# An output projection made of seven products of halves in place of eight, and the three products of a hidden block kept together, in an f32 kernel of attention and MLP

## The chip, the cores and the metric

One of the eight cores of a Trainium2 chip. The time is device microseconds (us) of one execution. The engines: TensorE (PE: matmuls; PEld: its loads of weights, which overlap the matmuls), VectorE (DVE), ScalarE (ACT), GpSimd (POOL), SyncE (SP, which issues DMAs here).

## The reference, cut to what matters

An HGRN2 attention over 4 x 768 tokens and 8 heads of 48 gives x of 3072 x 384. An MLP follows; the change touches only its last product.

```python
def _moe_ref(x, w_in, w_out):
    h = x @ w_in                                   # 3072 x 384 @ 384 x 2048
    g = h * (1.0 / (1.0 + np.exp(-1.702 * h)))
    return (g @ w_out).astype(np.float32)          # 3072 x 2048 @ 2048 x 384
```

Everything is f32.

## The kernel before

Tokens are taken in 12 units of 256. Each unit has an attention part (many small matmuls of 48 or 64 rows, which wait for each other through VectorE and ScalarE) and an MLP part (large matmuls, which wait for little). TensorE's order is written by hand: between two attention parts it runs a measured share of the MLP of an older unit, so that the large matmuls fill the attention's waits. VectorE's and ScalarE's order in the late part is a scheduler's. Units 0 to 2 go through the MLP in blocks while w_in and w_out are still being fetched and turned from f64 to f32; units 3 to 11, the late ones, run whole.

```python
    def mlp_h(n, ffs, g):                 # h of one 128-row block: three products over c
        def one(ff, c):
            ...
            nc.tensor.matmul(ph, lhsT=w_in[:, c, ff * P:(ff + 1) * P], rhs=xTs[n][:, c, :], start=(c == 0), stop=(c == NK - 1))
            if c == NK - 1:
                nc.scalar.activation(sg, ph, AF.Sigmoid, scale=1.702)
                nc.vector.tensor_tensor(g[ff // FG][:, ff % FG, :], ph, sg, ALU.mult)
        return [(U, lambda ff=ff, c=c: one(ff, c), ...) for ff in ffs for c in range(NK)]

    def mlp_o(n, ffs, g, done):           # o of 128 tokens: 16 products of 384 columns
        def one(tt, ff):
            if ff == ffs[0]:
                t["po"] = ps.tile([P, DM], F32, tag="mm", bufs=4, ...)
            nc.tensor.matmul(t["po"], lhsT=g[ff // FG][:, ff % FG, tt * P:(tt + 1) * P], rhs=w_out[:, ff, :],
                             start=(ff == ffs[0]), stop=(ff == ffs[-1]))
            if ff == ffs[-1]:
                done(tt, t["po"])         # ScalarE copies po out, then the store
        ...
```

The h, the o and some attention transposes take turns on four PSUM banks (tag "mm"). [Cuts are marked with "...".]

Of the kernel before, what the change touches and what calls it, by code (L numbers as in the profile page):

```python
# [9 lines left out]
F32 = mybir.dt.float32  # L10
I32 = mybir.dt.int32
U32 = mybir.dt.uint32
AF = mybir.ActivationFunctionType
ALU = mybir.AluOpType
# [9 lines left out]
def kernel(  # L24
# [7 lines left out]
    moe_w_out: bass.AP,  # L32
    out: bass.AP,
):



# [19 lines left out]
    nc = tc.nc  # L57
    B, H, S, D = q.shape
    DM = H * D
    DFF = moe_w_in.shape[1]  # L60
    P = 128
    C = 64
    G = 128
    U = 256
# [7 lines left out]
    NK = DM // P  # L72
    NFF = DFF // P
    FG = 4
    PAIRS_AHEAD = 3
# [9 lines left out]
    wp = ctx.enter_context(tc.tile_pool(name="wp", bufs=2))  # L85
    mlp = ctx.enter_context(tc.tile_pool(name="mlp", bufs=2))
    ps = ctx.enter_context(tc.tile_pool(name="ps", bufs=1, space=bass.MemoryType.PSUM))
# [43 lines left out]
    X = const.tile([P, 3, NX], F32, name="X")  # L131
# [8 lines left out]
    w_out = const.tile([P, NFF, DM], F32, name="w_out")  # L140
# [7 lines left out]
    pieces, pairs = [], []  # L148
    for r in range(NGR):
        ffs = range(r * FG, (r + 1) * FG)  # L150
        for ff in ffs[::2]:
            f = slice(ff * P, (ff + 2) * P)
# [8 lines left out]
    NPC = 2 * FG  # L161
# [68 lines left out]
    def convert():  # L230

        if state["begin"] < len(pairs) and len(todo) <= NOP:
            begin_pair(state["begin"])
            state["begin"] += 1
        if todo and todo[0]:
            todo.pop(0)()
        if todo and todo[0] is None:
            todo.pop(0)
            state["done"] += 2
            fetch_weights()  # L240
# [360 lines left out]
        return (begin_f, begin, begin_k, begin_gates), parts  # L601


    xTs = {}

    def width(n):

        return U + (n == NALL - 1)

    def mlp_h(n, ffs, g):  # L610
        t = {}

        def one(ff, c):
            if c == 0:
                if ff % FG == 0:
                    g[ff // FG] = mlp.tile([P, FG, width(n)], F32, tag="g", name=f"g_{n}_{ff}", bufs=6)
                t["ph"] = ps.tile([P, width(n)], F32, tag="mm", name=f"h_{n}_{ff}", bufs=4)
            ph = t["ph"]
            nc.tensor.matmul(  # L619
                ph, lhsT=w_in[:, c, ff * P:(ff + 1) * P], rhs=xTs[n][:, c, :], start=(c == 0), stop=(c == NK - 1)  # L620
            )
            if c == NK - 1:
                sg = mlp.tile([P, width(n)], F32, tag="sg", name=f"sg_{n}_{ff}")
                nc.scalar.activation(sg, ph, AF.Sigmoid, scale=1.702)  # L624
                nc.vector.tensor_tensor(g[ff // FG][:, ff % FG, :], ph, sg, ALU.mult)  # L625
                if width(n) > U:

                    by = g[ff // FG][:, ff % FG, U:]
                    if ff == 0:
                        g["last"] = mlp.tile([P, 1, DM], F32, tag="sum", name="sum_last", bufs=3)  # L630
                        nc.vector.tensor_scalar(g["last"][:, 0], w_out[:, 0, :], by, None, op0=ALU.mult)
                    else:
                        nc.vector.scalar_tensor_tensor(
                            g["last"][:, 0], w_out[:, ff, :], by, g["last"][:, 0], op0=ALU.mult, op1=ALU.add
                        )
        return [(U, lambda ff=ff, c=c: one(ff, c), ff // FG * NPC + ff % FG + 1) for ff in ffs for c in range(NK)]

    def mlp_o(n, ffs, g, done):

        t = {}  # L640

        def one(tt, ff):
            if ff == ffs[0]:
                t["po"] = ps.tile([P, DM], F32, tag="mm", name=f"o_{n}_{tt}_{ff}", bufs=4)
            nc.tensor.matmul(  # L645
                t["po"], lhsT=g[ff // FG][:, ff % FG, tt * P:(tt + 1) * P], rhs=w_out[:, ff, :],
                start=(ff == ffs[0]), stop=(ff == ffs[-1]),
            )
            if ff == ffs[-1]:
                done(tt, t["po"])  # L650
        return [(DM, lambda tt=tt, ff=ff: one(tt, ff), (ff // FG + 1) * NPC) for tt in range(U // P) for ff in ffs]

    def store(n, tt, o):
        r0 = n * U + tt * P - 1
        nc.sync.dma_start(out=out[max(r0, 0):r0 + P, :], in_=o[1:] if r0 < 0 else o)

    def mlp_unit(n):
        g = {}

        def done(tt, po):  # L660
            if tt == 0:
                g["o"] = mlp.tile([P, U // P, DM], F32, tag="osb", name=f"osb_{n}", bufs=1)
            o = g["o"][:, tt]
            nc.scalar.copy(o, po)  # L664
            store(n, tt, o)

        def last_token():
            po = ps.tile([P, DM], F32, tag="mm", name="o_last", bufs=4)
            nc.tensor.matmul(po[:1], lhsT=ones, rhs=g["last"][:, 0], start=True, stop=True)
            nc.scalar.copy(g["last"][:1, 0], po[:1])  # L670
            nc.sync.dma_start(out=out[NALL * U - 1:, :], in_=g["last"][:1, 0])
        o = mlp_o(n, range(NFF), g, done)
        if width(n) > U:
            o.insert(NFF, (DM, last_token, 0))
        return mlp_h(n, range(NFF), g) + o

    sums = {}

    def mlp_block(n, r):

        g, ffs = {}, range(r * FG, (r + 1) * FG)

        def done(tt, po):
            if r == 0 and tt == 0:
                sums[n] = mlp.tile([P, U // P, DM], F32, tag="sum", name=f"sum_{n}", bufs=3)
            acc = sums[n][:, tt]
            if r == 0:
                nc.scalar.copy(acc, po)
            else:
                nc.vector.tensor_tensor(acc, acc, po, ALU.add)  # L690
            if r == NGR - 1:
                store(n, tt, acc)
        return mlp_h(n, ffs, g), mlp_o(n, ffs, g, done)
# [10 lines left out]
    def parts_of(n):  # L704

        parts = list(units[n][1])
        _, inter = parts.pop()
        if n:
            kind, scores = parts[0]
            _, ahead = units[n - 1][1][-1]  # L710
            parts[0] = kind, lambda: (ahead(), scores())
        if n < N_TURN:

            def with_v(l):
                kind, fn = parts[l]
                return kind, lambda: (fn(), load_vl(n, l) if n == 0 or l else None)
            parts[:NL] = [with_v(l) for l in range(NL)]
        if n + 1 < NALL:
            begin_f, begin, begin_k, begin_gates = units[n + 1][0]
            i = len(parts)  # L720
            if n + 1 < N_FILL:

                parts.append(("K", lambda: (begin_k(), begin_gates(), load_vl(n + 1, 0) if n + 1 < N_TURN else None)))
                parts.insert(i - 4, ("B", begin))
                parts.insert(i - 5, ("B", begin_f))
            else:
                kind, states = parts.pop()
                parts += [("B", begin_k), (kind, lambda: (states(), begin_gates()))]
                parts.insert(i - 3, ("B", lambda: (begin_f(), begin())))
        else:  # L730
            parts.append(("W", inter))
        return parts

    def merge(n, fill, columns, share, pieces=0, hold=0, by=1.0):



        parts = parts_of(n)
        total = sum(share(kind) for kind, _ in parts)
        converting = {"W": 3, "T": 3, "B": 1} if n < N_FILL - 1 else {"W": 3, "V": 4, "S": 3, "T": 1, "B": 1}  # L740
        total_ops = sum(converting.get(kind, 0) for kind, _ in parts)
        held = sum(share(kind) for kind, _ in parts[:hold])
        at = at_ops = done = ops = 0
        for kind, fn in parts:
            ready = state["done"]
            fn()
            at += share(kind)
            at_ops += converting.get(kind, 0)
            n_ops = min(int(pieces * NOP * at_ops / (by * total_ops)), pieces * NOP) - ops
            ops += n_ops  # L750
            first, n_columns = done, max(0, columns * (at - held) / (total - held) - done)

            def some(end):
                nonlocal done
                while fill and done < end and fill[0][2] <= ready:
                    w, emit, _ = fill.pop(0)
                    emit()
                    done += w
            for i in range(n_ops):
                some(first + n_columns * i / n_ops)  # L760
                convert()
            some(first + n_columns)
# [4 lines left out]
    UNIT = NFF * NK * U + U // P * NFF * DM  # L767
# [14 lines left out]
    fill = []  # L782
# [8 lines left out]
    for n in range(3, NALL):  # L791
        fill += mlp_unit(n)
    for n in range(4, NALL):
        merge(n, fill, UNIT, steady)
    for _, emit, _ in fill:
        emit()

# [28 lines left out]
```

## Time and profile before

| | before |
|---|---|
| median of the three runs | 677.96 us (677.47 to 679.17) |
| span in the profile | 674.0 us |
| TensorE busy | 652.6 us, 97% |
| VectorE busy | 378.4 us, 56% |
| passes of h, distance from start to start | 216 ns for 256 columns |
| passes of o, distance from start to start | 322 ns for 384 columns |
| one late unit, from the start of an attention y to the next unit's | 50.94 us |

Each attention part has one group of matmuls that adds the old state to its output ("y<-X,st", L562). Its first start, read from the trace, divides the run into twelve stretches. I call these starts y1 to y12. From y5 to y11 they come every 50.94 us in the kernel before, all the same to 0.01 us.

The prediction below shows the lines of the profile and how they are read.

### The profile page before, as it was taken

Reading aid. Unit: us, or ns where it says so; the run is one execution under the profiler, and the core shown is the slowest. Engines: PE = TensorE matmul, PEld = TensorE weight load, DVE = VectorE, ACT = ScalarE, POOL = GpSimd, SP = SyncE. Lnnn points to the kernel's source line nnn. Section 1 sums busy time; section 2 is a strip of 40 time slices with the busy share of each in tenths; the row PEclk is TensorE's granted clock in tenths of the full one; section 3 lists DMA queues with packets and bytes.
Section 4 is the critical chain, followed back from the end, with each engine's and each line's share of the span. In section 5 each row is a group of like instructions: output and inputs, shape, how many; then the busy total and the mean of one; then the engine's idle time right before and its main releaser. Section 6 shows DMA issues by size and latency. Waiting matters only on the chain.

```text
span 674.0 us, 19354 instructions
## 1 busy us (share of the span) xinstructions
PE 652.6 (97%) x8514; PEld 486.5 (72%) x8514; DVE 378.4 (56%) x675; ACT 226.4 (34%) x459; POOL 50.3 (7%) x116
## 2 busy tenths in 40 slices
PE   5879999999999999999999999999999999999997
PEld 4656766757777886886886886876886786786774
DVE  3999877887666546545546546445446444430440
ACT  4564443343134233333333233233233233231210
POOL 3020020010002002002002002002002001000000
PEclk9789999999999999999999999999999999999999
DMA  8877973571063535415415415415414103001000
GB/s 193 226 192 193 240 160 89 152 185 37 24 159 107 154 66 149 109 38 148 115 33 152 110 37 148 113 37 144 115 37 115 37 24 84 15 1 36 13 1 24
DMA packets 67551, 67.62 MB, mean 100 GB/s; under 512 B 30410, under 2 KB 61290, under 8 KB 67466
## 3 DMA queue, kind: packets, MB, share of 16 engines
q1 hardware_dynamic: 67466, 66.38, 38.6%
q8 instruction: 67, 1.10, 0.7%
q14 instruction: 18, 0.15, 0.1%
HBM read 56.92 MB, written 8.65 MB: 97 GB/s over the span
## 4 chain that ended last, share of the span: by engine, by line
PE 89%; DVE 7%; ACT 2%; issue 1%; DMA 1%; SPq 0%; DVEq 0%; ACTq 0%
PE h L619 37%; PE o L645 35%; PE sc L383 5%; PE y L447 5%; PE t L338 2%; PE y L562 2%; PE tkn L504 1%; PE sc L522 1%; DVE s L218 1%; DVE A L409 1%; DMA xT<-yT 1%; PE tv L283 1%; ACT yT L570 1%; DVE X L436 1%; DVE X L438 1%
## 5 line engine op out<-in xcount | busy, mean ns | idle before, releaser
L619 PE MATMUL h<-xT,w_in 128*128 128x256 f32 (+1 forms) x1152 | 261.1, 382 | 1.1 <-DVE sum L690 0.8
L645 PE MATMUL o<-w_out,g 128*128 128x384 f32 x768 | 259.6, 491 | 0.9 <-DVE g L625 0.9
L619 PEld LDWEIGHTS h<-xT,w_in 128*128 128x128 f32 x1152 | 215.8, 190 | 36.8 <-issue 3.5
L645 PEld LDWEIGHTS o<-w_out,g 128*128 128x128 f32 x768 | 143.0, 190 | 94.5 <-issue 2.2
L625 DVE TENSOR_TENSOR g<-h,sg 128x256 f32<-128x256 f32 (+1 forms) x192 | 80.8, 422 | 133.1 <-ACT sg L624 132.6
L624 ACT ACTIVATE sg<-h 128x256 f32<-128x256 f32 (+1 forms) x192 | 73.2, 383 | 169.4 <-PE h L619 164.1
L422 ACT COPY Kc<-X 128x512 f32<-128x512 f32 x69 | 45.9, 666 | 123.7 <-DVE X L438 87.3
L438 DVE TENSOR_TENSOR X<-X,tot 128x1024 f32<-128x1024 f32 x45 | 55.2, 1226 | 54.8 <-PE sc L383 50.1
L409 DVE TENSOR_TENSOR A<-sc,masks 128x512 f32<-128x512 f32 x72 | 46.7, 679 | 0.0
L326 DVE STREAM_TRANSPOSE X<-raw 128x1024 f32<-128x1024 f32 x18 | 36.7, 2039 | 16.7 <-PE y L562 13.9
L447 PE MATMUL y<-A,vl 64*48 64x64 f32 x2304 | 41.7, 219 | 0.0
L447 PEld LDWEIGHTS y<-A,vl 64*48 64x48 f32 x2304 | 36.8, 122 | 5.3 <-issue 5.0
L375 POOL TENSOR_TENSOR tot<-F 128x512 f32<-128x512 f32 x12 | 12.5, 1039 | 340.5 <-DVE st L539 327.9
L383 PE MATMUL sc<-X,Kc 48*64 48x64 f32 x1344 | 29.0, 224 | 6.8 <-ACT Kc L422 4.6
L383 PEld LDWEIGHTS sc<-X,Kc 48*64 48x64 f32 x1344 | 24.6, 138 | 13.8 <-ACT Kc L422 7.2
L570 ACT COPY yT<-y 48x512 f32<-48x512 f32 x48 | 27.8, 580 | 20.0 <-PE y L562 19.4
L331 ACT ACTIVATE F<-F 128x1024 f32<-128x1024 f32 x9 | 9.5, 1057 | 49.0 <-DVE F L326 49.0
L375 POOL TENSOR_TENSOR tot<-tot 128x256 f32<-128x256 f32 (+4 forms) x60 | 23.7, 395 | 4.7
L542 DVE TENSOR_TENSOR st<-st,sc 128x192 f32<-128x192 f32 x44 | 15.6, 354 | 15.1 <-PE sc L522 13.7
L338 PE MATMUL t<-ident,raw 128*64 128x128 f32 x288 | 19.6, 298 | 4.4 <-DMA raw<-in_f_logit_dram 4.4
L338 PEld LDWEIGHTS t<-ident,raw 128*64 128x64 f32 x288 | 18.4, 153 | 7.0 <-issue 6.1
L664 ACT COPY osb<-o 128x384 f32<-128x384 f32 x18 | 8.6, 478 | 41.5 <-PE o L645 41.5
(66 smaller groups left out, 385.0 us busy)
## 6 DMA issues: line engine op xcount, KB each, us to landing
vl<-v_tok SPq DMA_DIRECT2D x60, 192.0 KB, 2.8
bits<-in_moe_w_out_dram SPq DMA_DIRECT2D x8, 768.0 KB, 9.8
bits<-in_moe_w_in_dram SPq DMA_DIRECT2D x8, 576.0 KB, 7.9
v_tok<-in_v_dram SPq DMA_DIRECT2D x10, 384.0 KB, 4.3
vn<-v_tok SPq DMA_DIRECT2D x10, 384.0 KB, 6.0
xT<-yT SPq DMA_DIRECT2D x24, 144.0 KB, 2.7
raw<-in_f_logit_dram SPq DMA_DIRECT2D x18, 192.0 KB, 3.9
raw<-in_q_dram SPq DMA_DIRECT2D x18, 192.0 KB, 3.1
```

The lines of the kernel that those rows point to most:

```text
L326: nc.vector.transpose(out.rearrange("p (a i j) -> p a j i", a=NP, j=R), raw[:, j].rearrange("p a (j d) -> p (a j) d", j=R)[:, :, :32],)
L338: nc.tensor.matmul(pt[h * HS:(h + 1) * HS, jj, :], lhsT=by_pair[j][:, h, x:x + HS], rhs=ident, start=True, stop=True)
L375: nc.gpsimd.tensor_tensor(tn, t2[:, :, 0], t2[:, :, 1], ALU.mult)
L383: nc.tensor.matmul(out[g * HS:(g + 1) * HS, h, a, :], lhsT=lhs(h, a * U + g * G), rhs=rhs(h, a * U + g * G), start=True, stop=True,)
L409: nc.vector.tensor_tensor(A[:, :, c:c + w].rearrange("p h (x t) -> p h x t", t=64), t["sc"][:, :, c:c + w].rearrange("p h (x t) -> p h x t ...
L422: nc.scalar.copy(c.rearrange("p (n m) -> p n m", m=m), X[:, j, :NA].rearrange("p (n two m) -> p n two m", two=2, m=m)[:, :, hf, :],)
L438: nc.vector.tensor_tensor(qk, qk, by, ALU.mult)
L447: nc.tensor.matmul(dst(h, g, a), lhsT=vls[n, u][g * 64:(g + 1) * 64, (2 * a + h) * D:(2 * a + h + 1) * D], rhs=A(h, g, a), start=(start an ...
L619: nc.tensor.matmul(ph, lhsT=w_in[:, c, ff * P:(ff + 1) * P], rhs=xTs[n][:, c, :], start=(c == 0), stop=(c == NK - 1))
L624: nc.scalar.activation(sg, ph, AF.Sigmoid, scale=1.702)
L625: nc.vector.tensor_tensor(g[ff // FG][:, ff % FG, :], ph, sg, ALU.mult)
L645: nc.tensor.matmul(t["po"], lhsT=g[ff // FG][:, ff % FG, tt * P:(tt + 1) * P], rhs=w_out[:, ff, :], start=(ff == ffs[0]), stop=(ff == ffs[ ...
```

## The change

The intent: a product of 2 x 2 blocks by 2 x 2 blocks needs eight products of blocks, or seven with some sums (Strassen's method, here in a form that shares sums). The blocks are two halves of the tokens and two of the 2048 hidden rows in g, and two halves of the hidden rows and two of the 384 columns in w_out. TensorE saves one product in eight; VectorE pays with sums of 128x512 over g in each unit (eight), and once with sums over the quarters of w_out (T1 to T4). Four banks X, W, Y, Z hold the products; three of the four are used twice or added to.

```diff
+    def sums_of_b():                       # T1 to T4, ten sums on VectorE, once
+        sub = lambda *x: nc.vector.tensor_tensor(*x, ALU.subtract)
+        ...
+    def sums_of_a(n, g, b):                # six sums a unit, as the blocks of g arrive
+        if b < 2:
+            tt(g["S", j][:, :, t1], g[j][:, :, t0], g[j][:, :, t1], ALU.subtract)
+        else:
+            tt(g[j][:, :, t1], g[j][:, :, t1], g[j + 2][:, :, t1], ALU.add)
+            tt(g["S", j][:, :, t0], g[j][:, :, t1], g[j][:, :, t0], ALU.subtract)
+    def last_sum(n, g):                    # two more, once the product p2 has read the old block
+        ...
+        def p6():
+            nc.vector.tensor_tensor(row("u2"), t["p1"], t["Y"], ALU.add)
+        def p7():
+            nc.vector.tensor_tensor(row("u3"), t["p1"], t["Y"], ALU.add)
+            ...
+        products = (
+            ("X", a(0, 0), b(0, 0), p1, True), ("W", a(1, 1), T_(4), p4, True), ("X", a(0, 1), b(1, 0), p2, False),
+            ("Y", s(0), T_(2), p6, True), ("Z", a(1, 0), T_(1), p5, True), ("Y", s(1), T_(3), p7, False),
+            ("Z", a(0, 1), b(1, 1), p3, False),
+        )
...
-        return [(U, lambda ff=ff, c=c: one(ff, c), ...) for ff in ffs for c in range(NK)]
+        return [(NK * U, lambda ff=ff: [one(ff, c) for c in range(NK)], ...) for ff in ffs]
...
-        o = mlp_o(n, range(NFF), g, done)
+        o = mlp_o7(n, g)
...
-        return mlp_h(n, range(NFF), g) + o
+        return mlp_h(n, range(NFF), g, True) + o
```

In "products" the last field says whether the product starts a bank afresh (True) or is added to what is there (False). Each is 8 matmuls of 192 columns. Not shown: the share of the MLP that runs between two attention parts is counted anew for the fewer columns, and the program gives out the sums of w_out two at a time in the attention part of unit 4.

## The prediction

> **What bounds the kernel now.** I read the page first, for the share of each engine and for the slices of time:
>
> ```profile
> PE 652.6 (97%) x8514; PEld 486.5 (72%) x8514; DVE 378.4 (56%) x675; ACT 226.4 (34%) x459; POOL 50.3 (7%) x116
> ...
> PE   5879999999999999999999999999999999999997
> PEld 4656766757777886886886886876886786786774
> DVE  3999877887666546545546546445446444430440
> ...
> PE h L619 37%; PE o L645 35%; PE sc L383 5%; PE y L447 5%; PE t L338 2%; PE y L562 2%; PE tkn L504 1%; PE sc L522 1%; DVE s L218 1%; DVE A L409 1%; DMA xT<-yT 1%; PE tv L283 1%; ACT yT L570 1%; DVE X L436 1%; DVE X L438 1%
> ```
>
> TensorE (PE) is at 9 in nearly every slice, and the chain that ended last runs through h (37%) and o (35%), both on TensorE. A busy PE need not be at its peak, so I then took one middle stretch of 51 us, about one unit of 256 tokens, from the busy time by windows:
>
> ```profile
> core 0: us, PE busy (x) PEld busy (x) DVE busy (x) ACT busy (x) POOL busy (x), PEclk, DMA share, GB/s
> 310.00:361.00 51.00, 51.00 (x682) 38.49 (x680) 25.92 (x38) 16.93 (x35) 4.03 (x8) 1.00 0.39 100
> ```
>
> There is no hole in TensorE there and its clock is full; VectorE (DVE) has half the time free. All PE waits over 0.15 us that I found in the trace lie before 152 us. So from there on, a us of TensorE work removed is a us off the end, unless a new wait appears. The cost of one matmul is not its duration (they overlap) but the distance from start to start. The timeline gives it:
>
> ```profile
> 599.21 0.60 PE L504 MATMUL tkn<-ident,X 128*128 128x128 f32 x4
> 599.65 2.32 PE L619 MATMUL h<-xT,w_in 128*128 128x256 f32 x10
> 648.74 10.48 PE L645 MATMUL o<-w_out,g 128*128 128x384 f32 x32
> ```
>
> A run of n lasts (n-1) distances and one duration. For o, with the group's own median duration of 0.486 us: (10.48-0.486)/31 = 322.4 ns for 384 columns. For h: (2.32-0.379)/9 = 215.7 ns for 256. An f32 product is two such passes (the 1152 h records are 12 units x 48 products x 2), so o takes 32 x 2 = 64 passes a unit, 64 x 322.4 = 20.63 us.
>
> **What the Trainium skill says.** "TensorE: Matmul & The Clock Gate", section "Back-to-back issue gap", gives N/2.4 + 2.5 ns per warm matmul. The trace agrees if each f32 pass takes two cycles a column: 2x256/2.4+2.5 = 215.8 and 2x384/2.4+2.5 = 322.5, both within 0.2 ns of what I read. By that line a pass of 192 columns takes 162.5 ns; the straight line through the two measured points gives 162.4. The same page, section "LDWEIGHTS (loading the stationary operand)", gives columns/1.2, 107 ns for 128. The trace seems to differ, for a load is shown with 190 ns:
>
> ```profile
> L619 PEld LDWEIGHTS h<-xT,w_in 128*128 128x128 f32 x1152 | 215.8, 190 | 36.8 <-issue 3.5
> L645 PEld LDWEIGHTS o<-w_out,g 128*128 128x128 f32 x768 | 143.0, 190 | 94.5 <-issue 2.2
> ```
>
> But where h follows the 128-column transposes of k (first pair of lines of the timeline above), the loads start about 109 ns apart, (0.60-0.273)/3, and by single records the first load of h starts at 599.541, its matmul at 599.648, 107 ns later, and the next one comes 219 ns after that, only 3 late. So 190 is a latency, and about 110 ns the pace of loads. A pass of 192 columns hides that.
>
> "VectorE: DVE Perf Modes", section "The TRN2 errata", gives (N+151)/0.96 ns for an f32 tensor_tensor: 691 ns at 512, 357 at 192. The trace has 685 for X<-X,tot at 512 and 354 for the state updates at 192: agreed.
>
> **The change part by part.**
>
> Removed and added on TensorE: for the nine late units (3 to 11), 64 passes of 384 columns become 7 products x 8 blocks x 2 = 112 passes of 192, at 162.5 ns = 18.20 us. Saved 20.63-18.20 = 2.43 us a unit, 21.9 us in nine. All of it lies where PE has no holes. Weights are loaded 112 times instead of 64, hidden as argued. The switches between h or o and the small attention matmuls (about 93 ns lost each: 309 instead of 216 from a last h pass to a first sc) stay as many, one for each part of attention, so I give nothing for the three products of an h kept together; it only stops a half-filled bank from being held over an attention part.
>
> Added on VectorE, a unit: eight sums over 128x512 (8 x 0.69 = 5.5 us) and five over 192 columns (5 x 0.355 = 1.8 us), 7.3 us. ScalarE: four copies of 192 columns for two of 384, some +0.3 us (an estimate). VectorE would be busy 26+7.3 = 33 of about 48.5 us: still not the bound by sum. Once, ten sums of w_out's quarters: 6 of 768 columns and 4 of 384, 6 x 0.96 + 4 x 0.55 = 7.9 us.
>
> Moved: the bound by sum is not enough, because VectorE works in order. I went through the order of instructions of both kernels for each place where TensorE waits for VectorE or ScalarE.
>
> - The fourth accumulator, Y, is used twice: S x T2, then 8 blocks of Z, then S' x T3 added into the same bank. The second use must wait until VectorE has taken the first (u2 = p1+Y). In VectorE's order u2 stands behind: two corrections of a (which wait for the product before the attention's y), the transpose of q, the state, two promotions of X and the mask. In the kernel before, the same row runs like this, o having restarted at 363.37:
>
> ```profile
> 362.58 2.06 DVE L326 STREAM_TRANSPOSE X<-raw 128x1024 f32<-128x1024 f32 x1 [2.12 <-PE y L562]
> 364.49 0.34 DVE L539 TENSOR_TENSOR st<-st,tot 128x192 f32<-128x192 f32 x1
> 364.75 1.20 DVE L438 TENSOR_TENSOR X<-X,tot 128x1024 f32<-128x1024 f32 x1
> 365.88 1.27 DVE L409 TENSOR_TENSOR A<-sc,masks 128x512 f32<-128x512 f32 x2
> 367.32 1.24 DVE L438 TENSOR_TENSOR X<-X,tot 128x1024 f32<-128x1024 f32 x1 [0.17 <-ACT Qc L422]
> ```
>
> It ends at 368.56, 5.2 us after the restart. The two corrections (1.3 us) can start about 1.1 us before y ends and push it by some 0.15 us. Then u2 takes 0.35. So Y is free at 5.2+0.15+0.35 = 5.7 us, while TensorE arrives after 16 blocks x 2 x 0.1625 = 5.2 us: a new wait of 0.5 us. Units 3, 5, 6 and 8 have this; 4 and 7 have no state step in the row (0.3 us less, wait 0.2); 9 has no transpose, 10 and 11 no attention in the way: none. Sum 4 x 0.5 + 2 x 0.2 = 2.4 us.
>
> - X's and Z's second use wait for ScalarE copies that have 2.6 us of other products to run in: none. The four matmul banks: the next unit's first h's take X's and W's, long free; the fourth takes Z's some 3 us after its sum should be done: none.
> - The scheduler draws the sums of w_out up into the early stage, near 153 us, and puts the first two (1.9 us) ahead of the first gelu product of a block, where TensorE already waits for banks that VectorE empties:
>
> ```profile
> PE h L619 <- DVE sum L690: 0.8, 1, 0.8
> ```
>
> I put 1.2 us of new PE wait there (a choice between nothing and the full 1.9); the rest falls in idle VectorE time.
>
> At the end a sum of 192 columns takes the place of a copy of 384 (0.48 us) before the last store: about -0.1, left out. Sum: 677.96 - 21.9 + 2.4 + 1.2 = 659.7 us, a fall of 2.7%.
>
> **The rivals.**
> - Loads become the bound: if the 190 ns were the pace, o would take 112 x 0.190 = 21.3 us a unit, 0.65 more than now, 684 us in all. For: PEld's duration is what the page shows, and nothing of exactly this shape (two-pass f32, 128x128 weights, under 190 ns apart) runs in the kernel but at the transposes' border. Against: that border, and the 109 ns pace of the transposes.
> - VectorE becomes a bound in stretches: the wait for Y grows to 1 us or more in all units, and h's banks are emptied late because of the sums between the gelu products. For: in-order engine, 7 us more, the transposes of 2 us. Against: VectorE idles about 0.9 us of each 1.3 us of h. It would leave a gain of 10 to 14 us, 664 to 668.
> - No new wait: if VectorE's row runs 0.5 us sooner than I think, 656.
> - The early stage (to 152 us, VectorE at 8 or 9 tenths) shifts with the changed order of h, either way by 1 to 2 us.
>
> **Range and chances.** The saving is arithmetic on a well supported pace; the waits can only be 0 to about 8 us. Fast end 655, slow end 666. The 2% line is 664.4; below it lies most of that range, so faster 0.84, within 2% 0.15, slower 0.01 (the load rival, which I hold nearly refuted).
>
> **What would show it.** Distances of 162 to 163 ns in o's passes (190 or more refutes the main step). A unit period near 48.5 to 49.0 us instead of 50.9. In PE's waits a new line of o for the u2 sum on VectorE, some 0.2 to 0.6 us each, six times; a wait near 153 us. Wrong if o's starts are uneven at every bank change, if the six waits are above 1 us, or if PE shows waits for gelu products in every unit.

## The result, and the profile after

| | before | after |
|---|---|---|
| median of the runs | 677.73 us (4 runs, 677.47 to 679.17) | 659.96 us (4 runs, 658.95 to 662.17) |
| span in the profile | 674.0 us | 656.8 us |
| VectorE busy | 56% | 68% |
| a late unit (y5 to y11, mean) | 50.94 us | 48.72 us |
| y3 to y4 | 68.54 us | 70.19 us |

Faster, ratio 0.9738 with a 95% interval of 0.9708 to 0.9768. A ratio here is the mean time of one kernel's runs over that of the other's of the same rounds, so not quite the ratio of the medians quoted beside it. Executions over 1.5% slower than the fastest of the same kernel are left out of the means. The kernel before has one run more here than when the prediction was written.

The page of the changed kernel, the same rows as shown for the kernel before (busy time; busy tenths in 40 slices; the chain that ended last):

```profile
PE 630.0 (96%) x8946; PEld 541.2 (82%) x8946; DVE 444.7 (68%) x802; ACT 230.2 (35%) x477; POOL 53.4 (8%) x116
...
PE   6669999989999999999999999999999999999997
PEld 5546667766678689989989989989989989989997
DVE  2988887788887757657658658558558557553571
...
PE 84%; DVE 9%; ACT 2%; issue 2%; DMA 1%; SPq 0%; DVEq 0%; ACTq 0%
PE h L727 37%; PE o L755 7%; PE o_X L704 7%; PE o_Y L704 7%; PE o_Z L704 7%; PE sc L384 5%; PE y L448 4%; PE o_W L704 4%; PE t L339 2%; PE y L563 2%; PE sc L523 1%; PE tkn L505 1%; DVE X L439 1%; DMA xT<-yT 1%; DVE s L219 1%
```

TensorE is still the chain. The o of the late units now stands under o_X, o_W, o_Y and o_Z; L755 is the o of the early blocks. VectorE went up in every late slice, by one to three tenths, and is far from full by this count. PEld is up from 72% to 82% although the kernel is faster: there are more loads, and they still hide. That they hide is seen in the timeline of the last unit, after the attention is over:

```profile
608.11 2.76 PE L704 MATMUL o_Y<-T,S 128*128 128x192 f32 x16
610.71 2.76 PE L704 MATMUL o_Z<-w_out,g 128*128 128x192 f32 x16
```

Sixteen passes from 608.11 to 610.71: 2.60/16 = 162.5 ns each, as worked out beforehand. A load of 190 ns that had to end first would not fit.

Where did 17.1 us of the profiled span come from? By the ruler of the y's:

| stretch | before | after | difference |
|---|---|---|---|
| start to y3 | 139.60 | 142.03 | +2.4 |
| y3 to y4 | 68.54 | 70.19 | +1.65 |
| y4 to y5 | 51.38 | 48.42 | -2.96 |
| y5 to y11, six units | 305.66 | 292.31 | -13.35 |
| y11 to y12 | 45.14 | 42.65 | -2.49 |
| y12 to the end | 63.66 | 61.22 | -2.44 |

So from y4 on the change gives 21.2 us, and the part before y4 takes some of it back. A word of care on y3 to y4: in the trace 144 passes of h lie in this stretch after the change and 142 before it, and in y4 to y5 it is 96 against 98. So 2 x 0.2157 = 0.43 us of the +1.65 is work that only changed places, and 1.23 us (unrounded) is lost; t_pool and h_only below show where this comes from.

Two new waits were forecast. The first, at the second use of Y, is in the trace in this form (VectorE's timeline of one late unit, then TensorE's; the columns are start, duration, engine, line, operation and tiles, count, and in brackets the idle time before it with what ended it):

```profile
357.52 1.29 DVE L650 TENSOR_TENSOR g<-g,S 128x512 f32<-128x512 f32 x2
359.20 2.06 DVE L327 STREAM_TRANSPOSE X<-raw 128x1024 f32<-128x1024 f32 x1 [0.38 <-PE y L563]
361.10 0.34 DVE L540 TENSOR_TENSOR st<-st,tot 128x192 f32<-128x192 f32 x1
361.37 1.22 DVE L439 TENSOR_TENSOR X<-X,tot 128x1024 f32<-128x1024 f32 x1
362.51 1.27 DVE L410 TENSOR_TENSOR A<-sc,masks 128x512 f32<-128x512 f32 x2
363.96 1.24 DVE L439 TENSOR_TENSOR X<-X,tot 128x1024 f32<-128x1024 f32 x1 [0.18 <-ACT Qc L423]
365.10 0.34 DVE L679 TENSOR_TENSOR u<-p,o_Y 128x192 f32<-128x192 f32 x1
```

```profile
359.98 2.87 PE L704 MATMUL o_Y<-T,S 128*128 128x192 f32 x16
362.68 2.76 PE L704 MATMUL o_Z<-T,g 128*128 128x192 f32 x16
365.50 2.87 PE L704 MATMUL o_Y<-T,S 128*128 128x192 f32 x16
```

Z starts at 362.68 and its 16 passes would let the second Y start at 365.28. It starts at 365.50, just after u2 ends at 365.44. TensorE's waits do not list this, because the modelled ends of the last passes cover the hole; the distance from start to start does. By single records, this start comes 380 ns after the one before it, where 163 is normal, and the second pass of the product comes 267 ns after the first, 104 more than normal.

The row also shows the place where my estimate of its length failed: the two corrections (L650) start at 357.52 and are over at 358.81, and the transpose then idles 0.38 us until y has ended. They push nothing. (The first of them starts while the product before y is still running, until 358.07: it needs only the first half of that product.)

The second wait forecast, in the early stage, is the first sums of w_out ahead of the first gelu product of a block. VectorE before, then after:

```profile
152.53 0.54 DVE L690 TENSOR_TENSOR sum<-sum,o 128x384 f32<-128x384 f32 x1
152.99 0.55 DVE L227 TENSOR_TENSOR w_in<-a,s 128x384 f32<-128x384 f32 x1
153.46 0.41 DVE L625 TENSOR_TENSOR g<-h,sg 128x256 f32<-128x256 f32 x1
```

```profile
155.41 0.55 DVE L793 TENSOR_TENSOR sum<-sum,o 128x384 f32<-128x384 f32 x1
155.87 1.82 DVE L622 TENSOR_TENSOR T<-w_out 128x768 f32<-128x768 f32 x2
157.61 0.41 DVE L733 TENSOR_TENSOR g<-h,sg 128x256 f32<-128x256 f32 x1
```

From the sum to the first g it was 0.93 us and is now 2.20. TensorE's timeline of the changed kernel shows what that costs:

```profile
154.61 2.96 PE L727 MATMUL h<-xT,w_in 128*128 128x256 f32 x12 [0.94 <-DVE sum L793]
158.08 0.70 PE L727 MATMUL h<-xT,w_in 128*128 128x256 f32 x2 [0.51 <-DVE g L733]
```

The first of these waits was there before (0.78 us, for a bank that the same sum empties); the second is new.

### The profile page after: what moved, and what is told of

Same layout as the page of the kernel before. It is cut to its first block, busy times and chain, and to the rows that moved or that the text cites. A ratio compares the mean times of both kernels' runs of the same rounds, so it can differ in the third digit from the quotient of the medians.

```text
span 656.8 us, 20370 instructions
## 1 busy us (share of the span) xinstructions
PE 630.0 (96%) x8946; PEld 541.2 (82%) x8946; DVE 444.7 (68%) x802; ACT 230.2 (35%) x477; POOL 53.4 (8%) x116
## 4 chain that ended last, share of the span: by engine, by line
PE 84%; DVE 9%; ACT 2%; issue 2%; DMA 1%; SPq 0%; DVEq 0%; ACTq 0%
PE h L727 37%; PE o L755 7%; PE o_X L704 7%; PE o_Y L704 7%; PE o_Z L704 7%; PE sc L384 5%; PE y L448 4%; PE o_W L704 4%; PE t L339 2%; PE y L563 2%; PE sc L523 1%; PE tkn L505 1%; DVE X L439 1%; DMA xT<-yT 1%; DVE s L219 1%
## 5 line engine op out<-in xcount | busy, mean ns | idle before, releaser
L755 PE MATMUL o<-w_out,g 128*128 128x384 f32 x192 | 66.4, 493 | 0.0
L755 PEld LDWEIGHTS o<-w_out,g 128*128 128x128 f32 x192 | 35.3, 190 | 22.8 <-issue 1.5
L704 PE MATMUL o_X<-w_out,g 128*128 128x192 f32 x288 | 51.9, 329 | 0.0
L704 PE MATMUL o_Y<-T,S 128*128 128x192 f32 x288 | 51.1, 331 | 0.1
L704 PEld LDWEIGHTS o_Y<-T,S 128*128 128x128 f32 x288 | 46.5, 190 | 2.6 <-DVE u L679 1.3
L704 PEld LDWEIGHTS o_X<-w_out,g 128*128 128x128 f32 x288 | 47.3, 190 | 0.9
L376 POOL TENSOR_TENSOR tot<-tot 128x256 f32<-128x256 f32 (+4 forms) x60 | 26.9, 448 | 4.7
L704 PE MATMUL o_Z<-w_out,g 128*128 128x192 f32 x144 | 26.6, 331 | 0.0
```

Source lines behind the costliest of these rows:

```text
L376: nc.gpsimd.tensor_tensor(tn, t2[:, :, 0], t2[:, :, 1], ALU.mult)
L704: nc.tensor.matmul(t[bank], lhsT=lhs(f), rhs=rhs(f), start=(new and f == 0), stop=(f == HF - 1), skip_group_check=True,)
```

## The experiments

My theory: the gain is the number of passes times 162.5 ns and nothing else; VectorE's sums cost nothing by themselves except at two places, the second use of Y and the sums of w_out in the early stage; keeping an h together is worth nothing by itself. The rivals: narrow passes or h's order bring the gain; loads come near to binding; VectorE's sums hold up h or the attention.

Between neighbours such as after_again, own_bank and t_pool the intervals overlap; there it is the stretches of the traces that tell them apart, and these came out the same to 0.01 us in three profiles of the changed kernel.

All twelve runs at a glance. "before" is the median of the kernel before in the same rounds. "unit" is the mean of y5 to y11, and "y3-y4" the stretch of the early stage, both from the run's profile.

| run | median us | before | ratio (95% interval) | unit | y3-y4 |
|---|---|---|---|---|---|
| after_again | 659.92 | 678.39 | 0.972 (0.970 to 0.974) | 48.72 | 70.19 |
| split_h | 660.92 | 678.39 | 0.9742 (0.9727 to 0.9758) | 48.99 | 69.77 |
| own_bank | 658.96 | 678.39 | 0.9707 (0.9685 to 0.9729) | 48.50 | 70.18 |
| t_pool | 657.77 | 678.39 | 0.9699 (0.968 to 0.9718) | 48.72 | 69.42 |
| h_only | 679.24 | 678.19 | 1.0012 (0.9992 to 1.0031) | 50.94 | 69.42 |
| o_2x192 | 680.25 | 678.19 | 1.0029 (1.0007 to 1.0051) | 51.10 | 68.56 |
| o_4x96 | 748.99 | 678.19 | 1.104 (1.1009 to 1.1071) | 58.80 | 68.53 |
| no_sums | 658.91 | 678.19 | 0.9709 (0.969 to 0.9728) | 48.71 | 70.20 |
| best | 657.71 | 677.79 | 0.971 (0.9683 to 0.9738) | 48.51 | 70.26 |
| sums_double | 663.33 | 677.79 | 0.9788 (0.9769 to 0.9807) | 49.43 | 70.19 |
| own_pool | 656.52 | 678.51 | 0.968 (0.9663 to 0.9697) | 48.55 | 69.43 |
| after_third | 660.28 | 678.51 | 0.9727 (0.9708 to 0.9747) | 48.72 | 70.19 |

**after_again: the changed kernel, unchanged.**

> The changed kernel again, unchanged, as the partner of the runs beside it. Expected 660 us, within 1.5; six waits of the second Y, together 1.3 us, and 47.9 us from one unit's attention y to the next, as in its first profile. If the early stage (up to the y of the fourth attention unit, at 212.2 us in the first profile against 208.1 before) comes out elsewhere by more than 1 us, that stage varies from run to run and part of its 4 us is no effect of the change.

659.92 us. The unit and the stretch y3 to y4 came out the same to 0.01 us, so these two can be compared to a tenth. The first three stretches cannot: y3 was at 142.03 us in the first profile and at 143.73 here, and over all runs, with orders that differ little up to there, y1 alone was anywhere from 41.5 to 46.4. The +2.4 us before y3 in the table above is therefore not put down to the change. The 1.65 us from y3 to y4 is an effect. (The 47.9 us a unit expected here and in split_h is the mean over all eight stretches from y4 to y12 of the first profile, 383.4/8, the shorter last one included. By the ruler of this document the same profile has 48.72.)

**o_2x192: eight products of halves.** The kernel before, with each product of the late o cut in two.

```diff
-            nc.tensor.matmul(t["po"], lhsT=g[...], rhs=w_out[:, ff, :], ...)
+            for x in range(0, DM, DM // k):        # k = 2
+                nc.tensor.matmul(t["po"][:, x:x + DM // k], lhsT=g[...], rhs=w_out[:, ff, x:x + DM // k], ...)
```

> The kernel before, with each product of o in the late units done as two of 192 columns: eight products of halves, no Strassen, no sums. Theory (a pass of 192 costs 162.5 ns, so only their number counts): 128 passes x 162.5 = 20.80 us a unit against 20.63, 0.17 more, 1.5 us in nine units: 679.9. Rival (the narrow passes are what saves time, or loads bind at 190): 660, or 20.63 to 24.3 us a unit and 711.

680.25 us, 51.10 us a unit: 0.16 more than before, where 0.17 was expected. The distance of the passes was 163 ns (64 of them in 10.56 us). Narrow passes are no gain; what counts is that seven are fewer than eight, 112 passes against 128. The result of this run and the next is wrong (relative errors of 0.152 and 0.187). The Trainium skill, "PSUM — Partial Sum Buffer", section "The four PSUM rules", has the reason: a first matmul of a group clears the accumulation marks of the whole bank, so two groups open at once in one bank cannot both have one. Here the second piece's start wipes the first piece's, and one block in sixteen is lost in half the columns of nine units in twelve. By an estimate that takes the blocks as independent that is a relative error of sqrt(9/12 x 1/2 x 1/16) = 0.153, and for the next run, with three quarters of the columns, 0.188. Both agree. The number and size of the passes, which this run is about, are the same with a right result.

**o_4x96: four pieces of 96.** The same with k = 4.

> The same with four pieces of 96 columns, to find the floor that the loads of weights set under narrow products. By the columns alone a pass would take 82.5 ns: 256 x 82.5 = 21.1 us a unit, 682. If loads set the pace at 110 ns (theory): 28.2 us a unit, 7.5 more, 68 in nine units: 746. If at 190: 48.6 us a unit, 930.

748.99 us. The passes came 112 ns apart, where 96 columns by themselves would take 82.5. The row of the groups:

```profile
L646 PE MATMUL o<-w_out,g 128*128 128x96 f32 (+1 forms) x2496 | 330.1, 292 | 0.9 <-DVE g L625 0.9
L646 PEld LDWEIGHTS o<-w_out,g 128*128 128x128 f32 x2496 | 295.8, 192 | 26.7 <-issue 2.2 <-DVE g L625 1.5
```

The load is still shown with 192 ns each, and yet the pace is 112. So the duration of a load in the profile is not its pace, and this run shows the floor that a narrower Strassen would meet: 192 columns (162.5 ns) are above it, 128 columns (109, an estimate by the line) would lie just at it. That it is the loads that set this floor, and not something else in each pass, is argued: the loads are paced at 112 ns as well, but no run takes them away.

**h_only: an h kept together, alone.**

```diff
-        return [(U, lambda ff=ff, c=c: one(ff, c), ...) for ff in ffs for c in range(NK)]
+        return [(NK * U, lambda ff=ff: [one(ff, c) for c in range(NK)], ...) for ff in ffs]
```

> The kernel before with the three products of an h kept together, nothing else. Theory (worth nothing by itself; in the run of Strassen alone its lack cost 0.25 us a unit only because it moved a product behind the attention's y): same as before, within 1 us, 50.9 us a unit. Rival (it is a gain of its own, 1 us or more, for every kernel): 677 or less against 678.4.

679.24 us, the unit exactly as before, no gain. But the stretch y3 to y4 is 0.88 us longer than before. Of this 0.43 is no loss: here too two passes of h have moved from y4 to y5 (which is 0.43 us shorter, 50.95 against 51.38) into this stretch, because the shares between the attention parts are cut elsewhere. The other 0.45 us comes from a wait at the head of the stretch: the matmuls of y wait for a sum of the state on VectorE (L542), and one of them comes 0.68 us after the one before it instead of 0.20. In all nine profiles with h kept together this distance is 0.68, in all five with h in pieces 0.18 to 0.21. Whether the time before y3 is shorter by as much cannot be told in its scatter. In the prediction this part stood at nothing.

**split_h: Strassen alone.** The changed kernel with that line put back.

> Strassen's seven products alone: the three products of an h are again three separate pieces of TensorE's order. Theory (the seven products carry the gain, keeping an h together gives nothing): 660 us, within 1.5 of the changed kernel beside it, 47.9 us a unit. Rival (a bank held half filled over an attention part costs waits): slower than the changed kernel by 2 us or more, with waits of h for banks.

660.92 us against 659.92 beside it: a difference of one us, inside what I allowed. The unit says more: 48.99, 0.27 longer. TensorE, then VectorE, in one unit:

```profile
360.24 0.59 PE L704 MATMUL o_X<-w_out,g 128*128 128x192 f32 x2
360.67 2.76 PE L704 MATMUL o_Y<-T,S 128*128 128x192 f32 x16
363.27 2.76 PE L704 MATMUL o_Z<-T,g 128*128 128x192 f32 x16
366.35 0.92 PE L704 MATMUL o_Y<-T,S 128*128 128x192 f32 x4 [0.32 <-DVE u L679]
```

```profile
365.35 0.68 DVE L650 TENSOR_TENSOR g<-g,S 128x512 f32<-128x512 f32 x1
365.95 0.35 DVE L679 TENSOR_TENSOR u<-p,o_Y 128x192 f32<-128x192 f32 x1
```

With separate products the shares between the attention parts come out one o product different: a last X product falls behind the attention's matmuls. The correction that must wait for it then stands in VectorE's order right ahead of u2, so u2 comes 0.60 us later in its row; TensorE comes 0.33 us later to the second Y, by the two passes that moved behind, and the wait grows by the difference, 0.27 us. In the Strassen kernel the second part of the change thus does have a use, some 6 x 0.27 = 1.6 us in the late units. It has no price early there: 69.77 against 70.19 us is the 0.43 us of moved work again.

**own_bank: no wait at Y.** The seventh product starts a bank of its own.

```diff
-            nc.vector.tensor_tensor(row("u3"), t["p1"], t["Y"], ALU.add)
+            nc.vector.tensor_tensor(row("u3"), t["u2"], t["V"], ALU.add)
-            ... ("Y", s(1), T_(3), p7, False),
+            ... ("V", s(1), T_(3), p7, True),
```

> The seventh product gets a bank of its own, and u3 is u2 plus it, so no product waits until VectorE has read Y. Theory (the second use of Y costs 1.3 us in six units): those waits are gone and it takes 1.3 us less than the changed kernel, 658.7. Rival (the wait only moves to the bank that comes next): same as the changed kernel, with a wait at V or at a following h of the same size.

The wait is gone and none takes its place:

```profile
364.71 2.76 PE L704 MATMUL o_Z<-T,g 128*128 128x192 f32 x16
367.31 2.76 PE L704 MATMUL o_V<-T,S 128*128 128x192 f32 x16
369.91 0.81 PE L704 MATMUL o_Z<-w_out,g 128*128 128x192 f32 x4
```

From Z to V it is 2.60 us, 16 passes of 162.5. The unit is 48.50 us, 0.215 less, 1.29 us in six units; from the trace of the changed kernel, the excess over 163 ns at the second Y and at the pass behind it sums to 1.28 us for units 3 to 8. The median is 1.0 us less than the changed kernel's, in a profile whose y1 happened to be the latest of all, at 46.40; the runs' times alone would not show this gain. And 50.943 - 48.503 = 2.44 us is what a unit gains when no wait is in it: 64 x 322.4 - 112 x 162.5 = 2.43.

**t_pool: the sums of w_out on GpSimd.**

```diff
-        sub = lambda *x: nc.vector.tensor_tensor(*x, ALU.subtract)
+        sub = lambda *x: nc.gpsimd.tensor_tensor(*x, ALU.subtract)
```

> The ten sums of the quarters of w_out are made by GpSimd, which is busy 8%, in place of VectorE. Theory (these sums, drawn up into the early stage, make TensorE wait there): 1.2 us less than the changed kernel, up to 3, with the early y of the fourth attention unit sooner by as much. Rival (the early stage lost its time to another order or by chance): within 0.5 us of the changed kernel. A third way: GpSimd and VectorE hinder each other, and the early stage is longer.

657.77 us. The stretch y3 to y4 is 69.42, 0.77 less, and the wait of an h for g near 158 us is gone. GpSimd needs twice as long for a sum (1.9 us for 768 columns against 0.95) and nobody waits. So these sums cost 0.77 us in the changed kernel and not 1.2, and 69.42 is just what h_only has without any sums. The rest of the 2.1 us in the medians lies before y3, where the runs scatter.

**no_sums: the late units without the eight sums over g** (wrong result; S is replaced by a block of g).

> The changed kernel without the eight sums over a in each late unit; the result is wrong on purpose. Theory (VectorE has the time for them; the wait at Y comes from the transpose of q behind y, not from them): within 1 us of the changed kernel, 659 to 660, with 48.7 us a unit and the waits at Y still there. Rival (they hold up h's banks or the attention): 2 us or more faster, the period of a unit under 48.5.

48.71 us a unit against 48.72. All 5.5 us a unit of extra VectorE work cost 0.01 us. The median is 1.0 us less than after_again's in other rounds, with y3 at 141.21; the late part gives no reason for it.

**sums_double: eight more sums a unit** (four sums made three times; the result stays right).

```diff
+            for _ in range(3):
                 tt(g["S", j][:, :, t1], g[j][:, :, t0], g[j][:, :, t1], ALU.subtract)
...
```

> The changed kernel with four of the eight sums over a made three times, eight more of 128x512 a unit, 5.2 to 5.5 us of VectorE; the result stays right. It asks how far VectorE is from being a bound. Theory (there is room, as the run without the sums was no faster a unit): 48.7 us a unit, and 660 us within 1. Rival (VectorE is near its limit where it also serves h and the attention): over 49.5 us a unit, 667 or more, with waits of h for g.

Neither: 49.43 us a unit, 663.33 us. My expectation of no cost fell. The place is again Y, and no h waits for g more than before:

```profile
366.31 2.76 PE L706 MATMUL o_Z<-T,g 128*128 128x192 f32 x16
369.84 2.87 PE L706 MATMUL o_Y<-T,S 128*128 128x192 f32 x16 [0.76 <-DVE u L681]
```

```profile
362.35 1.29 DVE L652 TENSOR_TENSOR g<-g,S 128x512 f32<-128x512 f32 x2
363.56 2.03 DVE L327 STREAM_TRANSPOSE X<-raw 128x1024 f32<-128x1024 f32 x1
```

The extra sums make the row in front of u2 late: the two corrections now start 0.7 us after y has begun and end at 363.64, 0.9 us after y has ended (362.74), and the transpose of q follows them without the idle 0.38 us. The first sums were free because VectorE waited there anyway; the next ones go straight into TensorE's wait. In the profile VectorE has room in every late slice, but this row has only a few tenths of a us.

**best: the own bank, GpSimd's sums, and h split again in the early blocks only.**

> What the runs point to, together: an own bank for the seventh product, the sums of w_out's quarters on GpSimd, and the three products of an h kept together only in the late units, where Strassen needs it, not in the early blocks. Theory: 1.3 us less for the waits at Y, 1.7 less in the stretch from the third to the fourth attention unit's y (68.5 us as in the kernel before, in place of 70.2): about 657 us, 48.5 us a unit. Rival: GpSimd's sums come late for the fourth unit's o, or the parts take each other's place: no faster than the changed kernel's 659.9.

A miss in its main point: y3 to y4 took 70.26 us, not 68.5. This time no work has moved, so 1.72 us is lost against the kernel before. The two early effects do not add. The wait at the head of the stretch is gone, but without the sums on VectorE and with h split, TensorE still waited 0.97 us for a bank near 154 us (0.78 in the kernel before) and for g near 157 and 159 us (1.2 us in two waits). My guess is that moving an item changes the order of VectorE's instructions there; that is not shown, and which order is good I did not find out. The late part came out as expected, 48.51.

**own_pool and after_third: the two edits that each held, and the changed kernel beside them.**

> The two edits that each held by itself, together, with h kept together everywhere as in the changed kernel: an own bank for the seventh product and the sums of w_out's quarters on GpSimd. If they add: 48.50 us a unit (as with the own bank) and 69.4 us from the third to the fourth attention unit's y (as with GpSimd's sums), together 2 us less than the changed kernel beside it. If the early stage comes out at 70.2 again, its order and not the sums decides there, and 1.3 us less is left.

> The changed kernel once more, as partner on the same chip: 659.9 within 1, 48.72 us a unit, 70.19 us from the third to the fourth attention unit's y.

Here they add: 69.43 us and 48.55 us a unit (one of the six periods was 0.25 us longer than the others; I did not follow it up). 656.52 us against 660.28 on the same chip, and the intervals of the ratios, 0.9663 to 0.9697 and 0.9708 to 0.9747, do not meet. The 3.8 us is more than the 2 us expected. The stretches from y3 on explain 1.8 us of it (0.76 and 6 x 0.17); the rest is before y3. This is the version with the lowest ratio, correct, and better than both kernels; that it is faster than t_pool alone (0.968 to 0.9718) is not shown by the times.

## Why the prediction was right or wrong

The time, 659.96 for 659.7, was right. Not all of its terms were, and that the sum came within 0.3 us is partly luck: the wait at Y was put 1.1 us too high, and about as much is lost before y3, for which there was no term.

- **The saving on TensorE (21.9 us): right.** 162.5 ns a pass, 2.43 us a unit, and a measured 2.44 where no wait disturbs it (own_bank). That loads would hide under 192 columns was right too, and o_4x96 gives the floor, 112 ns.
- **The new wait at the second use of Y (2.4 us): the mechanism was right, its size was not.** It measured 1.28 us. The step that failed is that the two corrections push the transpose of q by 0.15 us. They ended before y did (358.81, while the transpose waited until 359.20), because the first of them needs only the first half of the product before y. Two smaller terms were off by 0.1 us each: u2 starts before the promotion ahead of it has ended (365.10 and 365.20) and so ends 5.46 us after the restart instead of 5.7, and TensorE comes 0.1 later, at 5.3, because after the restart a second pass is 104 ns late. So TensorE's hole was 0.15 to 0.22 us in place of 0.5, and behind it another second pass is 0.1 us late, which I had not counted. The form was as forecast: units 3, 5, 6 and 8 have it, 4 and 7 have 0.04 and 0.1, 9 to 11 nothing.
- **The wait from the sums of w_out (1.2 us): the right size, but in the changed kernel from two causes instead of one.** y3 to y4 is 1.65 us longer, of which 0.43 is moved work and 1.23 is lost. With h split the sums alone lose as much, 69.77 - 68.54 = 1.24. In the changed kernel moving the sums off VectorE gives back 0.77; the other 0.45 is the wait of y that h_only has by itself. What each is worth depends on the order of the rest, as best showed.
- **Nothing for the three products of an h kept together: wrong.** It gains 1.6 us in the late units of the Strassen kernel, by the place at which the shares are cut. Early it costs 0.45 us in the kernel before; in the Strassen kernel the loss is the same with and without it (1.23 and 1.24).
- **VectorE has the time for the sums: right for what the change adds, with less to spare than the busy share says.** no_sums shows them free; sums_double shows that as much again costs 0.71 us a unit. (The ten sums of w_out are 8.0 us by the prediction's own numbers, not 7.9; the trace has 7.6.)
- **The rivals**: loads as the bound and h's banks emptied late are refuted by the distances and by no_sums. A shift of the early stage by its order happened.

In sum -21.9 + 1.28 + 1.23 = -19.4 from y3 on, and the profiles show -19.6. Most of the rest lies behind the last product, where a sum of 192 columns takes the place of a copy of 384: y12 to the end is 2.44 us shorter and its passes give 2.30, so about 0.1, as forecast and left out.

What the change does before y3 the two profiles compared (2.4 us) cannot say, with a scatter as large. The mean span is 676.5 us in 38 executions of the kernel before (the rounds of the experiments) and 657.9 in 13 of the changed kernel, 18.6 us less. From y3 on it is 19.6. By this estimate, which takes the late part to be as steady in every execution as in the profiles, about 1.0 us, give or take 0.7, is lost before y3. Its cause stays open.

## What to carry to other kernels

When one engine is the bound without holes, the distance from start to start of its instructions, as a line through two sizes, gives the worth of an arithmetic saving closely (here 2.43 us a unit for a measured 2.44); check with a direct run how narrow a pass may get before loads set the pace. What the other engine pays showed here not in its busy share but in the in-order row in front of the one result that the bound engine waits for: count that row against the time the bound engine takes to get there. And an accumulator that another engine must read before it is added to again can be a wait (0.04 to 0.32 us a unit here); a bank of its own and a sum that builds on the first took it away and cost nothing that the trace shows. Last, before a stretch between two marks is called longer, count the work in it: two passes of h on the other side of a mark looked like a loss of 0.43 us.

## What the Trainium skill lacked or had wrong

- "TensorE: Matmul & The Clock Gate", sections "Back-to-back issue gap" and "LDWEIGHTS (loading the stationary operand)", do not say what f32 takes; "FP8 and Floating Point Precision", section "TensorE Precision Notes", gives four passes for true FP32, without a time. In these runs an f32 product is recorded as two passes, each with its own load: 162.5 ns for 192 columns, 215.7 for 256, 322.4 for 384, that is 0.83 ns a column (two cycles at the first page's 2.4 GHz) and about 2.5 ns. The first section calls its line the gap of an isolated matmul and gives about 131 ns for N=512 in a stream of loads and matmuls; here the stream kept to the line, 215.7 ns for 256 f32 columns, which would be N=512. Passes with a load of 128 columns each came 112 ns apart in o_4x96, and 109 in the transposes of k, where the page's line for a load gives 107.
- The same page tells that loads are pulled ahead, not what a break costs. After a wait or a switch from the small attention matmuls the second f32 pass came 267 ns after the first instead of 163. I found this on no page.
- "Perfetto Trace Analysis", section "Identifying the Most-Contended Engine", takes the summed time of the loads over the window as a measure of how close TensorE is to its limit. Here the loads overlap in the trace, so the sum is 181% of the span before and 198% after; counted once where they overlap, as on the page of the profile, it is 72% and 82%. Both went up while the kernel became 2.6% faster and no load was waited for in the steady passes; each load is shown with 190 ns, but the pace can be 112.
